# One queue for the first loads, another order of transfers and statistics, and a new order of work on TensorE

## The chip, the cores and the metric

The kernel runs on one core of one Trainium2 chip. Its time is the device time of one execution, in microseconds. The engines are TensorE (PE: matmuls; PEld: its weight loads), VectorE (DVE), ScalarE (ACT), GpSimd (POOL) and SyncE (SP). SP issues DMAs and computes nothing; ACT can issue DMAs too.

## The reference

A layer norm without scale feeds two branches, and both are added to the input. S is 2048, D 448, H 16 heads of 28, F 1792; all inputs are bfloat16.

```python
xn = layernorm(x)                                   # (1, 2048, 448)
# branch A: linear attention with a softmax feature map
q, k, v = split(xn @ wqkv)                          # 16 heads of 28
pq, pk = q @ w_phi, k @ w_phi                       # per head
phi = lambda p: concat(softmax(p), softmax(-p))     # 56 features
kv, z = phi(pk).T @ v, phi(pk).sum(tokens)
A = ((phi(pq) @ kv) / (phi(pq) @ z + 1e-6)) @ wo
# branch B: feed-forward
B = silu(xn @ w1) @ w2
out = x + A + B
```

## The kernel before

**Tiles.** The 2048 tokens are 16 tiles of 128. D is contracted in pieces of 128 rows (the last piece overlaps the third, so that its upper 64 rows are the remainder); matmuls with 64 rows run in pairs on the two halves of PE.

**How the program is ordered.** Nothing is emitted directly. Every instruction is recorded as an operation with its engine, an assumed duration, the tiles it reads and writes, and a name; `schedule` (L218) then orders each engine by a list schedule over these assumptions, and waits are derived from the data dependences. All matmuls are emitted by one helper line (L469), all activations by L489, all plain loads by L503, all DMA transposes by L562. Two things bind the order by hand: `chain` (L883) makes the named operations of one engine follow each other, and the text `PLAN` (L334) lists the blocks of PE after the head; `strict` (L943) makes PE follow it.

**The loads.** x comes as x0, x1, x2 (tiles 2 and 3), x4, x8 and x12 (four tiles each). w1 comes in pieces named by their first column: w1_0 (256 columns, rows 0 to 383) with w1_0r (the remaining 64 rows, inside the last 128), w1_256r (those rows for columns 256 to 767), w1_256, w1_512, w1_768, w1_1280. wv, w2 and wo follow. w1_256 and w1_512 are issued by ACT, together with w_phi; all others by SP.

**The head.** Tiles 0 to 3 are normalised on DVE (`ln_tile`, L600): bnst (statistics), bnag (aggregate), ve on ACT (square root), rstd (reciprocal), xn (subtract and scale). PE transposes them through PSUM (tr0a, tr0, tr1, tr2, tr3), and ACT (tiles 0 to 2: ev0a, ev0, ev1, ev2) or DVE (tile 3: ev3) copies the result to `xnT`. Blocks F0, F1 and F2 of the up-projection are computed tile by tile in between: in the list at L905 the word `12` is block 1, tile 2; `10a` is block 1, tile 0, contraction steps one and two, `10b` the third.

**Tiles 4 to 15** are normalised with POOL in place of ACT and transposed by DMA, two tiles at a time: xnT_dma5 moves tiles 4 and 5, xnT_dma7 tiles 6 and 7, up to xnT_dma15. Eight transposes wT_dma0 to wT_dma7 bring q's and k's weights, which the fold multiplies with w_phi on PE. The chain at L932 fixes the order of x8, x12, wT and xnT on SP; SP issues in order and stops where an operation has to wait.

**Words of PLAN.** `aF12@0` is the first half of up-projection block 12 into banks 0 and 1, `bF12` its second half and eviction; block n holds column pair n mod 7 of token group n div 7 (512 tokens, so blocks 7 to 13 need tiles 4 to 7). v, k and q are projections of two tiles, f the fold, K the sums over tokens (they need POOL's `phik`), M their masking, s the scaling of q's features on POOL with their DMA transposes (`phqT` in the code, phT<-RA in the profile), U the attention product of a tile, after which DVE normalises (den, rden, o) and SP transposes o by DMA (vaug<-vaug in the profile). W is the output projection's three full pieces, R or r the remaining 64 rows, paired over tiles of odd and even slots by `finish_tiles` (L874), followed by the eviction (`out_ev`) and the store. F and Y are parts of the down-projection: `F4@0:2` is two of 14 steps of tile 4 in bank 0. E is the last tile.

Of the kernel before, what the change touches and what calls it, by code (L numbers as in the profile page):

```python
# [8 lines left out]
ACTF = mybir.ActivationFunctionType  # L9
# [131 lines left out]
class _Prog:  # L141
# [76 lines left out]
    def schedule(self):  # L218
# [55 lines left out]
        while done < n:  # L274
# [56 lines left out]
TAIL = {"act": 110.0, "dve": 85.0, "pool": 45.0}  # L331
SIGNAL = {("act", "pe"): 60.0, ("act", "dve"): 40.0, ("dve", "pe"): 100.0, ("dve", "sp"): 30.0, ("dve", "dve"): 34.0,
          ("pool", "pe"): 100.0}
PLAN = """aF3@4 bF3 aF6@0 aF4@2 bF6 av2@4 bF4 av0@6 bv2 bv0 aF12@0 aF8@2 aF9@4 bF8 bF9 aF11@6 bF12 bF11 f2@24 aF13@0 aF10@6 bF13  # L334
bF10 f0@24 aF5@0 aF7@6 bF5 bF7 ak2@4 bk2 av12@6 ak14@2 av10@0 bv12 bk14 bv10 ak4@4 av14@6 bk4 ak0@2 bv14 ak6@0 bk0 av8@4
bk6 ak8@6 bv8 bk8 Y2@3:2 Y2:12 av4@1 av6@6 ak10@4 bv4 bv6 bk10 ak12@2 aq4@0 bk12 K0-4 bq4 aq6@4 aq8@2 bq6 K4-8 aq0@0 bq8
aF17@4 bq0 bF17 s4 aF14@2 K8-10 bF14 aF19@0 K10-12 bF19 aF16@4 K12-16 aF23@2 bF16 bF23 aF27@0 M aF24@5 bF27 bF24 aF20@2
aF25@0 bF20 bF25 s6 aF26@5 aF22@3 bF26 bF22 aF21@0 aF18@5 bF21 aF15@2 bF18 aq12@0 s8 bF15 bq12 aq2@4 s0 U5 U4@6 Y1@3:3
Y1:2 Y1:9 F4@0:2 bq2 aq14@6 aq10@1 bq14 bq10 Y3@3:4 F8@5:9 Y3:10 F8:2 F8:1 F8:2 U8@1 F6@4:12 s2 s10 F4:3 F4:6 U7 F5@3:7
F4:3 U0@2 W4 s12 U6@6 F6:2 U9 U3@1 Y0@2:2 W8 F5:5 F5:2 U13 W5 r4 r5 Y0:8 U11 U12@6 F10@1:2 F10:6 U2@0 Y0:4 F10:1  # L340
F12@6:11 F7@2:3 W6 U10@0 F7:8 F7:3 F11@0:1 F11:4 F12:3 F10:5 W3@3 W0@7 W7 s14 W12 W10 R6,10,8,7 R3,0,12 F11:9 F14@4:7 U1
F13@5:1 F13:4 F13:9 F14:7 U14 W13 F9@2:3 W1@3 F9:4 U15 F9:7 W9 W11 W2@7 W14 R14,1 R9,2 R11,13 F15@61:14 E15"""


def bass_parallel_sum__linear_kernel_hedgehog__dense_activation_silu__prompt_kernel(
# [10 lines left out]
    S, D, H, DH, FF = 2048, 448, 16, 28, 1792  # L356
# [7 lines left out]
    KF = 384  # L364
# [11 lines left out]
    with es:  # L376
# [27 lines left out]
        w1_sb = flat[:, 0:4 * FF].rearrange("p (k f) -> p k f", k=4)  # L404
# [20 lines left out]
        warm_act = sb("warm_act", [128, 4], F32)  # L425
# [30 lines left out]
        def d_act(n):  # L456
            return n / 1.2 + 60.0
# [30 lines left out]
        def act(dst, src, func, n, name, scale=1.0, table=None, **keys):  # L488
            P.op("act", d_act(n), lambda e: e.activation(dst, src, func, scale=scale),  # L489
                 reads=[src], writes=[dst], table=table, name=name, **keys)  # L490
# [8 lines left out]
        def load(dst, src, name, eng="sp", lat=1700.0):  # L499
            n = 2  # L500
            for _, cnt in list(dst.ap):
                n *= cnt
            P.dma(lambda e: e.dma_start(out=dst, in_=src), n / 280.0, writes=[dst], name=name, eng=eng, lat=lat)  # L503
# [40 lines left out]
        load_x(1, 2)  # L544
        load_x(2, 4)
        load_w1(0, 256)
        load(w1_sb[:, 3, 256:768], B_w1[D - 128:D, 256:768], "w1_256r")
        for c in (256, 512):
            load(w1_sb[:, 0:3, c:c + 256], B_w1[0:KF, c:c + 256].rearrange("(k p) f -> p k f", p=128), f"w1_{c}", "act")
        load_x(4, 8)  # L550
        load_w1(768, 1280)
        load_w1(1280, FF)
# [47 lines left out]
        def ln_tile(t):  # L600
            xs = x_sb[:, t, :]
            sl = t % NXN
            P.op("dve", 590, lambda e: e.bn_stats(st6[:, t, :], xs), reads=[xs], writes=[st6[:, t, :]], name=f"bnst{t}", okeys_w=["ln"])  # L603
            P.op("dve", 170, lambda e: e.bn_aggr(mv[:, t, :], st6[:, t, :]), reads=[st6[:, t, :]], writes=[mv[:, t, :]], name=f"bnag{t}",
                 okeys_w=["ln"])
            if t < 4:
                P.op("act", 220, lambda e: e.activation(ve[:, t:t + 1], mv[:, t, 1:2], ACTF.Sqrt, bias=epst[:]),
                     reads=[mv[:, t, 1:2], epst[:]], writes=[ve[:, t:t + 1]], name=f"ve{t}", table="sqrt", okeys_r=["sq"])
                P.op("dve", 120, lambda e: e.reciprocal(rstd[:, t:t + 1], ve[:, t:t + 1]),
                     reads=[ve[:, t:t + 1]], writes=[rstd[:, t:t + 1]], name=f"rstd{t}")  # L610
            else:
                P.op("pool", 200, lambda e: e.tensor_scalar(ve[:, t:t + 1], mv[:, t, 1:2], EPS_LN, None, ALU.add),
                     reads=[mv[:, t, 1:2]], writes=[ve[:, t:t + 1]], name=f"ve{t}")
                P.op("pool", 570, lambda e: e.tensor_tensor(rstd[:, t:t + 1], ve[:, t:t + 1], neghalf[:], ALU.pow),  # L614
                     reads=[ve[:, t:t + 1], neghalf[:]], writes=[rstd[:, t:t + 1]], name=f"rstd{t}")

            def norm(dst, c0, c1, dur, tag=""):
                P.op("dve", dur, lambda e: e.tensor_scalar(dst, x_sb[:, t, c0:c1], mv[:, t, 0:1], rstd[:, t:t + 1], ALU.subtract, ALU.mult),  # L618
                     reads=[xs, mv[:, t, 0:1], rstd[:, t:t + 1]], writes=[dst], name=f"xn{t}{tag}")

            dstx = xnT[:, t, :, :]
            if t >= XN_DMA0:
                norm(xn_sb[:, sl, 0:KF], 0, KF, 370)
                norm(xn_sb[:, sl, KF:512], D - 128, D, 250)
                if t % 2:
                    dma_t(xnT[:, t - 1:t + 1, :, :].rearrange("p i k c -> p (i k) c"),
                          xn_sb[:, sl - 1:sl + 1, :].rearrange("p i c -> p (i c)"), 2200.0 if t < 8 else 1600.0, f"xnT_dma{t}", 1350.0)
                return

            def turn_over(k0, k1, b, tag):  # L630
                tps = bank16[b][:, 128 * k0:128 * k1].rearrange("p (k c) -> p k c", k=k1 - k0)
                transposes([(tps[:, kt - k0, :], xn_sb[:, sl, KS[kt]:KS[kt] + 128]) for kt in range(k0, k1)], f"tr{tag}")
                if t < 3:
                    act(dstx[:, k0:k1, :], tps, ACTF.Identity, 128 * (k1 - k0), f"ev{tag}")
                else:
                    copy(dstx[:, k0:k1, :], tps, 128 * (k1 - k0), f"ev{tag}")

            if t == 0:
                norm(xn_sb[:, sl, 0:256], 0, 256, 290, "a")
                norm(xn_sb[:, sl, 256:D], 256, D, 275)  # L640
                turn_over(0, 2, 4, "0a")
                turn_over(2, 4, 5, "0")
            else:
                norm(xn_sb[:, sl, 0:D], 0, D, 390)
                turn_over(0, 4, (7, 4, 5)[t - 1], str(t))
# [147 lines left out]
        UB = 7  # L793
        yts = {int(w[1:].split(":")[0].split("@")[0]) for w in PLAN.split() if w[0] == "Y"}
        ob_cnt = [0]
# [87 lines left out]
        def chain(names):  # L883
            byname = {o.name: o for o in P.ops}
            for a, b in zip(names, names[1:]):
                byname[b].odeps.add(byname[a].id)
                byname[b].odeps -= byname[b].deps
# [3 lines left out]
            ln_tile(t)  # L891
        fold()
        act(warm_act[:], ones_bf[:, 0:4], ACTF.Silu, 4, "silu_table", table="silu", okeys_w=["sq"])
        chain("bnst0 bnag0 bnst1 bnag1 rstd0 xn0a xn0 rstd1 xn1 bnst2 bnag2 bnst3 bnag3 rstd2 xn2 rstd3 xn3 ev3".split())
        chain("wphi warm_act w1_256 w1_512 ve0 ve1 ev0a ev0 ev1 ve2 ve3 ev2 silu_table".split())
        fold_loads()

        chunk = [(fp, c) for c in range(NCH) for fp in range(FP)]
# [3 lines left out]

        head = [F(0, 0), F(1, 2), F(2, AUX)]
        seq = []
        for word in "tr0a tr0 tr1 00a 00b 10a 01 10b 11 tr2 20 tr3 21 02 12 22 03 13 23".split():  # L905
            if word[0] == "t":
                seq.append(word)
                continue
            f, t = int(word[0]), int(word[1])
            n0 = len(P.ops)  # L910
            head[f][0](t * 128, t * 128 + 128, {"": (0, 1, 2), "a": (0, 1), "b": (2,)}[word[2:]])
            for n, o in enumerate(P.ops[n0:]):
                o.name = f"F{word}_{n}"
                seq.append(o.name)
# [3 lines left out]
            f[3]()  # L918
        for t in range(4, 8):
            ln_tile(t)  # L920
        chain("ev3 bnst4".split())
        block_mask(mask2[:], 2 * DH, 2)
        memset(vaug[:, :, :, DH], 1.0, 2150, "vaug1")
        def k_block(t, b0):
# [4 lines left out]

        for t in range(8, NT):  # L930
            ln_tile(t)
        chain("x8 wT_dma0 wT_dma1 wT_dma2 xnT_dma5 x12 xnT_dma7 wT_dma3 wT_dma4 wT_dma5 wT_dma6 wT_dma7 xnT_dma9 xnT_dma11 xnT_dma13 xnT_dma15 w2 "  # L932
              "wo0 wor0 wo1 wor1".split())
        memset(phq[:, :, :, KP:128], 0.0, 400, "phq0")
        late = max(o.id for o in P.ops if o.name == "xn15")
# [15 lines left out]
        open_kind = {"F": F, "v": v_block, "k": k_block, "q": q_block}  # L951
        for word in PLAN.split():
            n0 = len(P.ops)
            kind, arg = word[0], word[1:]
            if kind == "a":
                t, b = map(int, arg[1:].split("@"))
                blocks[arg[0], t] = open_kind[arg[0]](t, b)
                blocks[arg[0], t][2](0)
            elif kind == "b":
                f = blocks[arg[0], int(arg[1:])]  # L960
# [147 lines left out]
```

## Time and profile before

| | us |
|---|---|
| median of 8 runs | 150.23 (149.49 to 151.22) |
| the profiled execution's own time | 150.5 |
| its span in the trace | 149.2 |
| PE busy | 143.9 (96%) |
| DVE, ACT, POOL busy | 90.8, 71.2, 71.4 |

The granted clock of PE is full speed in every slice of the page. The span is from the first to the last recorded instruction. Times in the text are microseconds from its start. A matmul's recorded duration overlaps with the next one's, so the durations of PE rows are not added; starts are compared instead. A DMA row has the time from its issue to its landing. For the text, a hole is a stretch in which PE has nothing to do because it waits.

### The profile page before, as it was taken

What the parts mean: (1) busy time and instruction counts of PE and PEld (TensorE: products, weight loads), DVE (VectorE), ACT (ScalarE), POOL (GpSimd) and SP (SyncE); (2) the same over time, 40 slices, a digit from 0 to 9 for tenths busy, and PEclk for the clock granted to TensorE, in tenths of its full rate; (3) what the DMA queues carried; (4) which work ended last, traced back from release to release, by engine and by line L of the source; (5) the groups of instructions that cost most, each with busy time, mean ns of one, the idle gap of its engine ahead of it and who ended that gap; (6) DMA issues with size and microseconds to landing.
All of it is one profiled execution on the core that took longest, in us unless ns stands there. A gap on an engine that the chain in (4) does not pass through costs nothing.

```text
span 149.2 us, 3651 instructions
## 1 busy us (share of the span) xinstructions
PE 143.9 (96%) x1540; PEld 80.5 (54%) x1540; DVE 90.8 (61%) x189; ACT 71.2 (48%) x88; POOL 71.4 (48%) x82
## 2 busy tenths in 40 slices
PE   7799969999999999999999999999999999999994
PEld 7594435554554456656444454455565555455563
DVE  1968897343399966604995018998388620482255
ACT  3567755557999659899656685930000000000000
POOL 7107566510069999998899800896910000000000
PEclk9999999999999999999999999999999999999999
DMA  5999994989600000000089673068786984051135
GB/s 121 318 362 227 205 204 74 195 184 354 196 2 4 0 2 4 4 0 4 3 161 143 119 141 67 7 116 163 77 189 143 184 78 70 25 190 35 40 80 173
DMA packets 45297, 17.42 MB, mean 117 GB/s; under 512 B 36960, under 2 KB 44896, under 8 KB 45280
## 3 DMA queue, kind: packets, MB, share of 16 engines
q1 hardware_dynamic: 41712, 14.99, 49.3%
q10 hardware_dynamic: 3568, 2.20, 4.7%
q8 instruction: 12, 0.20, 0.6%
q14 instruction: 5, 0.04, 0.1%
HBM read 6.56 MB, written 1.84 MB: 56 GB/s over the span
## 4 chain that ended last, share of the span: by engine, by line
PE 93%; DMA 3%; issue 1%; SPq 1%; DVE 1%
PE psum L469 92%; DMA phT<-in_B_w_dram 3%; SPq L503 1%; DVE x_sb L856 1%; PE psum L484 0%
## 5 line engine op out<-in xcount | busy, mean ns | idle before, releaser
L469 PE MATMUL psum<-xnT,phT 64*128 64x512 bf16 (+1 forms) x428 | 44.9, 350 | 2.0 <-issue 1.2
L469 PE MATMUL psum<-w_sb,hT 128*128 128x448 bf16 (+1 forms) x238 | 45.4, 341 | 0.0
L489 ACT ACTIVATE hT<-psum 128x1024 bf16<-128x1024 f32 x28 | 27.2, 1023 | 15.6 <-PE psum L469 15.6
L469 PEld LDWEIGHTS psum<-xnT,phT 64*128 64x128 bf16 (+1 forms) x428 | 21.3, 95 | 21.9 <-issue 1.6
L774 POOL TENSOR_TENSOR RA<-Ek_sb,Rec 128x896 bf16<-128x896 bf16 x16 | 27.1, 1723 | 11.5 <-DVE Rec L739 11.5
L469 PEld LDWEIGHTS psum<-w_sb,hT 128*128 128x128 bf16 x238 | 22.2, 98 | 18.3 <-issue 1.5
L738 DVE TENSOR_REDUCE Rec<-Ek_sb 128x32 f32<-128x896 bf16 (+1 forms) x20 | 24.2, 1250 | 12.8 <-POOL Ek_sb L496 7.1
L469 PE MATMUL psum<-Wqk,xnT 64*128 64x432 bf16 x224 | 23.2, 343 | 0.1
L489 ACT ACTIVATE Ek_sb<-psum 128x864 bf16<-128x864 f32 x24 | 20.1, 910 | 2.6 <-PE psum L469 2.2
L748 POOL TENSOR_TENSOR Ek_sb<-Ek_sb,Rec 128x896 bf16<-128x896 bf16 x8 | 13.3, 1696 | 9.3 <-ACT phT L489 9.3
L469 PEld LDWEIGHTS psum<-Wqk,xnT 64*128 64x128 bf16 x224 | 10.7, 94 | 10.1 <-PE psum L469 0.9
L834 DVE TENSOR_SCALAR den<-psum 128x16 f32<-128x16 f32 x16 | 2.6, 162 | 19.7 <-PE psum L469 19.6
L748 POOL TENSOR_TENSOR phT<-phT,Rec 128x896 bf16<-128x896 bf16 x8 | 13.3, 1697 | 0.0
L856 DVE TENSOR_TENSOR x_sb<-psum,x_sb 128x448 bf16<-128x448 f32 (+1 forms) x13 | 7.1, 583 | 9.6 <-PE psum L469 9.6
L469 PE MATMUL psum<-wv,xnT 64*128 64x448 bf16 x112 | 12.4, 349 | 0.0
L603 DVE BATCH_NORM_STATS2 st<-x_sb 128x6 f32<-128x448 bf16 x16 | 9.7, 604 | 3.5 <-DMA x_sb<-in_A_x_dram 3.4
L469 PE MATMUL psum<-wo_sb,vaug 128*128 128x448 bf16 (+1 forms) x51 | 10.7, 341 | 0.0
L841 DVE TENSOR_TENSOR vaug<-psum,rden 128x448 bf16<-128x448 f32 x16 | 10.0, 625 | 0.7 <-DVE rden L836 0.2
L618 DVE TENSOR_SCALAR RA<-x_sb,mv,rstd 128x384 bf16<-128x384 bf16 (+4 forms) x29 | 8.9, 347 | 1.3 <-POOL rstd L614 1.2
L738 DVE TENSOR_REDUCE Rec<-phT 128x64 f32<-128x1792 bf16 x4 | 7.9, 1988 | 2.6 <-ACT phT L489 2.6
L489 ACT ACTIVATE vaug<-psum 128x896 bf16<-128x896 f32 x8 | 7.2, 927 | 3.3 <-PE psum L469 2.9
L739 DVE RECIPROCAL Rec<-Rec 128x32 f32<-128x32 f32 (+1 forms) x24 | 8.6, 392 | 0.1
(51 smaller groups left out, 105.0 us busy)
## 6 DMA issues: line engine op xcount, KB each, us to landing
out_dram<-x_sb ACTq DMA_DIRECT2D x15, 112.0 KB, 1.7
w_sb<-in_B_w_dram SPq DMA_DIRECT2D x1, 1568.0 KB, 7.7
x_sb<-in_A_x_dram SPq DMA_DIRECT2D x3, 448.0 KB, 5.1
phT<-in_B_w_dram SPq DMA_DIRECT2D x2, 384.0 KB, 6.0
wo_sb<-in_A_wo_dram SPq DMA_DIRECT2D x2, 336.0 KB, 8.5
phT<-in_B_w_dram ACTq DMA_DIRECT2D x2, 192.0 KB, 4.2
phT<-in_B_w_dram SPq DMA_DIRECT2D x3, 128.0 KB, 5.7
wv<-in_A_wqkv_dram SPq DMA_DIRECT2D x1, 336.0 KB, 6.6
```

The costliest lines, as they stand in the source:

```text
L469: r = e.matmul(dst, lhsT, rhs, start=st, stop=sp, skip_group_check=True)
L489: P.op("act", d_act(n), lambda e: e.activation(dst, src, func, scale=scale), reads=[src], writes=[dst], table=table, name=name, **keys)
L503: P.dma(lambda e: e.dma_start(out=dst, in_=src), n / 280.0, writes=[dst], name=name, eng=eng, lat=lat)
L603: P.op("dve", 590, lambda e: e.bn_stats(st6[:, t, :], xs), reads=[xs], writes=[st6[:, t, :]], name=f"bnst{t}", okeys_w=["ln"])
L618: P.op("dve", dur, lambda e: e.tensor_scalar(dst, x_sb[:, t, c0:c1], mv[:, t, 0:1], rstd[:, t:t + 1], ALU.subtract, ALU.mult), reads=[xs, ...
L738: P.op("dve", 50 + 967 * n, lambda e: e.tensor_reduce(R2, E4, AXL.X, ALU.add), reads=[E4], writes=[R2], name="Ssum")
L739: P.op("dve", 135 + 210 * n, lambda e: e.reciprocal(R2, R2), reads=[R2], writes=[R2], name="Rrec")
L748: P.op("pool", 1700, lambda e: e.tensor_tensor(E3, E3, Rk[:, :, None].broadcast_to([128, 32, DH]), ALU.mult), reads=[E3, Rk], writes=[E3], ...
L774: P.op("pool", 1700, lambda e: e.tensor_tensor(dst, Eq, Rq.rearrange("p (c j) -> p c j", c=CC)[:, :, :, None].broadcast_to([128, CC, 4, DH ...
L834: P.op("dve", 190, lambda e: e.tensor_scalar(den[:, uq, :], U3[:, :, DH], EPS_DEN, None, ALU.add), reads=[U3[:, :, DH]], writes=[den[:, uq ...
L841: P.op("dve", 620, lambda e: e.tensor_tensor(o3, U3[:, :, 0:DH], rden[:, uq, :, None].broadcast_to([128, H, DH]), ALU.mult), reads=[U3[:, ...
L856: P.op("dve", d_dve(cs.stop - cs.start), lambda e: e.tensor_tensor(res[:, cs], ob, addend[:, cs], ALU.add), reads=[ob, addend[:, cs]], wri ...
```

## The change

Six edits go together.

1. w1_256 and w1_512 are issued by SP, and w1_256r stands between them. SP's order is now x0, x1, x2, w1_0, w1_0r, w1_256, w1_256r, w1_512, x4, and so on.
2. The eviction of tile 2 (ev2) is two activations of 256 columns, ev2a and ev2.
3. In the head's list, block column 0 of F1 is no longer split, and tile 2's three blocks are split by contraction steps (`02a 12a 22a 02b 12b 22b`).
4. The chain on DVE is tied together: bnst4 stands before ev3, and bnag4 after it.
5. On SP, x12 is issued after wT_dma2 and before xnT_dma5; before, it stood between xnT_dma5 and xnT_dma7.
6. PLAN is replaced. Up to the fold it holds as many blocks as before, with F9, F8, F10 and F13 as the first of token group 1. Later, the order of Y, F, U and W words differs, and the remainders R run as one single tile and seven pairs, where before there were two singles and groups of 4, 3, 2, 2 and 2.

```diff
-PLAN = """aF3@4 bF3 aF6@0 aF4@2 bF6 av2@4 bF4 av0@6 bv2 bv0 aF12@0 aF8@2 aF9@4 bF8 bF9 aF11@6 bF12 bF11 f2@24 aF13@0 aF10@6 bF13
-bF10 f0@24 aF5@0 aF7@6 bF5 bF7 ak2@4 bk2 av12@6 ak14@2 av10@0 bv12 bk14 bv10 ak4@4 av14@6 bk4 ak0@2 bv14 ak6@0 bk0 av8@4
...
-F4:3 U0@2 W4 s12 U6@6 F6:2 U9 U3@1 Y0@2:2 W8 F5:5 F5:2 U13 W5 r4 r5 Y0:8 U11 U12@6 F10@1:2 F10:6 U2@0 Y0:4 F10:1
-F12@6:11 F7@2:3 W6 U10@0 F7:8 F7:3 F11@0:1 F11:4 F12:3 F10:5 W3@3 W0@7 W7 s14 W12 W10 R6,10,8,7 R3,0,12 F11:9 F14@4:7 U1
-F13@5:1 F13:4 F13:9 F14:7 U14 W13 F9@2:3 W1@3 F9:4 U15 F9:7 W9 W11 W2@7 W14 R14,1 R9,2 R11,13 F15@61:14 E15"""
+PLAN = """aF3@4 bF3 aF4@2 bF4 aF6@6 av2@0 av0@4 bF6 bv0 bv2 aF9@2 aF8@4 aF10@6 bF9 aF13@0 bF8 bF13 bF10 f2@24 aF5@0 aF7@6 bF5 bF7
+f0@24 aF12@0 aF11@6 bF12 bF11 ak2@4 bk2 av12@6 av10@0 ak14@2 bv12 bk14 bv10 ak4@4 av14@6 bk4 ak0@2 bv14 bk0 ak8@0 ak6@4
...
+F4:6 U8 F7@3:10 F7:3 U9@4 F7:1 F4:2 Y0:4 W5 W4 U3 W7 F9@6:1 aq14@4 R4 R5,7 bq14 F9:2 U1 F8@2:2 F8:12 U2 F9:11 s12 U12@4
+F6@5:5 W9 W3@1 U10@3 W1@0 F10@7:5 F6:9 W8 F14@3:3 F10:9 W6 W10 s14 R6,10 R3,9 R1,8 U13@4 F14:11 U14 F12@1:2 F11@2:8 U0@5
+W2@4 U11 F12:12 U15@0 F11:6 F13@6:5 W12 W14 W11 F13:9 W0@5 W13 R12,11 R14,0 R2,13 F15@70:14 E15"""
...
         load_w1(0, 256)
-        load(w1_sb[:, 3, 256:768], B_w1[D - 128:D, 256:768], "w1_256r")
         for c in (256, 512):
-            load(w1_sb[:, 0:3, c:c + 256], B_w1[0:KF, c:c + 256].rearrange("(k p) f -> p k f", p=128), f"w1_{c}", "act")
+            load(w1_sb[:, 0:3, c:c + 256], B_w1[0:KF, c:c + 256].rearrange("(k p) f -> p k f", p=128), f"w1_{c}")
+            if c == 256:
+                load(w1_sb[:, 3, 256:768], B_w1[D - 128:D, 256:768], "w1_256r")
         load_x(4, 8)
...
-                if t < 3:
+                if t == 2:
+                    act(dstx[:, 0:2, :], tps[:, 0:2, :], ACTF.Identity, 256, "ev2a")
+                    act(dstx[:, 2:4, :], tps[:, 2:4, :], ACTF.Identity, 256, "ev2")
+                elif t < 3:
...
-        chain("bnst0 bnag0 bnst1 bnag1 rstd0 xn0a xn0 rstd1 xn1 bnst2 bnag2 bnst3 bnag3 rstd2 xn2 rstd3 xn3 ev3".split())
-        chain("wphi warm_act w1_256 w1_512 ve0 ve1 ev0a ev0 ev1 ve2 ve3 ev2 silu_table".split())
+        chain("wphi warm_act ve0 ve1 ev0a ev0 ev1 ve2 ve3 ev2a ev2 silu_table".split())
...
-        for word in "tr0a tr0 tr1 00a 00b 10a 01 10b 11 tr2 20 tr3 21 02 12 22 03 13 23".split():
+        for word in "tr0a tr0 tr1 00a 00b 10 01 11 tr2 20 tr3 21 02a 12a 22a 02b 12b 22b 03 13 23".split():
...
-        chain("ev3 bnst4".split())
+        chain("bnst0 bnag0 bnst1 bnag1 rstd0 xn0a xn0 rstd1 xn1 bnst2 bnag2 bnst3 bnag3 rstd2 xn2 rstd3 xn3 bnst4 ev3 bnag4".split())
...
-        chain("x8 wT_dma0 wT_dma1 wT_dma2 xnT_dma5 x12 xnT_dma7 wT_dma3 wT_dma4 wT_dma5 wT_dma6 wT_dma7 xnT_dma9 xnT_dma11 xnT_dma13 xnT_dma15 w2 "
+        chain("x8 wT_dma0 wT_dma1 wT_dma2 x12 xnT_dma5 xnT_dma7 wT_dma3 wT_dma4 wT_dma5 wT_dma6 wT_dma7 xnT_dma9 xnT_dma11 xnT_dma13 xnT_dma15 w2 "
               "wo0 wor0 wo1 wor1".split())
```

More of the change, by code (lines that the diff above doesn't have):

```diff
@@ L333 @@
           ("pool", "pe"): 100.0}
-PLAN = """aF3@4 bF3 aF6@0 aF4@2 bF6 av2@4 bF4 av0@6 bv2 bv0 aF12@0 aF8@2 aF9@4 bF8 bF9 aF11@6 bF12 bF11 f2@24 aF13@0 aF10@6 bF13
-bF10 f0@24 aF5@0 aF7@6 bF5 bF7 ak2@4 bk2 av12@6 ak14@2 av10@0 bv12 bk14 bv10 ak4@4 av14@6 bk4 ak0@2 bv14 ak6@0 bk0 av8@4
[L336 to L339, printed above, removed]
-F4:3 U0@2 W4 s12 U6@6 F6:2 U9 U3@1 Y0@2:2 W8 F5:5 F5:2 U13 W5 r4 r5 Y0:8 U11 U12@6 F10@1:2 F10:6 U2@0 Y0:4 F10:1
-F12@6:11 F7@2:3 W6 U10@0 F7:8 F7:3 F11@0:1 F11:4 F12:3 F10:5 W3@3 W0@7 W7 s14 W12 W10 R6,10,8,7 R3,0,12 F11:9 F14@4:7 U1
-F13@5:1 F13:4 F13:9 F14:7 U14 W13 F9@2:3 W1@3 F9:4 U15 F9:7 W9 W11 W2@7 W14 R14,1 R9,2 R11,13 F15@61:14 E15"""
+PLAN = """aF3@4 bF3 aF4@2 bF4 aF6@6 av2@0 av0@4 bF6 bv0 bv2 aF9@2 aF8@4 aF10@6 bF9 aF13@0 bF8 bF13 bF10 f2@24 aF5@0 aF7@6 bF5 bF7
+f0@24 aF12@0 aF11@6 bF12 bF11 ak2@4 bk2 av12@6 av10@0 ak14@2 bv12 bk14 bv10 ak4@4 av14@6 bk4 ak0@2 bv14 bk0 ak8@0 ak6@4
+av6@6 bk6 bv6 bk8 Y2@2:1 Y2:9 Y2:1 Y2:3 av4@6 av8@0 ak10@4 bv8 bv4 bk10 ak12@2 aq4@0 bk12 K0-2 K2-4 bq4 aq6@4 aq8@2 bq6
+K4-8 aq0@0 bq8 s4 bq0 aF17@4 K8-10 bF17 aF14@2 K10-12 aF19@0 bF14 bF19 aF16@4 K12-16 aF23@2 aF27@0 bF23 bF27 bF16 M
+aF20@2 aF25@0 bF20 aF24@4 bF25 bF24 aF26@2 aF21@0 s6 aF18@6 aF22@4 bF21 s8 bF18 bF22 bF26 aF15@0 aq2@6 bF15 aq10@4 bq2
+aq12@2 bq10 bq12 Y1@0:14 s0 F5@1:4 Y3@6:11 F5:4 s2 F4@2:6 U4 Y3:3 s10 F5:1 F5:5 U5@3 U7@5 U6@4 Y0@6:1 Y0:3 Y0:2 Y0:4
+F4:6 U8 F7@3:10 F7:3 U9@4 F7:1 F4:2 Y0:4 W5 W4 U3 W7 F9@6:1 aq14@4 R4 R5,7 bq14 F9:2 U1 F8@2:2 F8:12 U2 F9:11 s12 U12@4
+F6@5:5 W9 W3@1 U10@3 W1@0 F10@7:5 F6:9 W8 F14@3:3 F10:9 W6 W10 s14 R6,10 R3,9 R1,8 U13@4 F14:11 U14 F12@1:2 F11@2:8 U0@5
+W2@4 U11 F12:12 U15@0 F11:6 F13@6:5 W12 W14 W11 F13:9 W0@5 W13 R12,11 R14,0 R2,13 F15@70:14 E15"""
 def bass_parallel_sum__linear_kernel_hedgehog__dense_activation_silu__prompt_kernel(
```

## The prediction

> **What bounds the kernel now.** I read the chain of work that ended last first, in order of time, because it says where TensorE (PE) stood still.
>
> ```profile
> 2.19 4.90 DMA phT<-in_B_w_dram
> ...
> 7.14 1.51 PE psum L469 x24
> ...
> 9.44 3.77 PE psum L469 x53
> ...
> 13.26 6.71 PE psum L469 x64
> 19.96 1.17 issue
> 21.14 14.83 PE psum L469 x150
> ...
> 36.01 110.84 PE psum L469 x1184
> 146.87 0.77 DVE x_sb L856 x2
> ```
>
> PE carries 92.5% of it. It waits in two places only: until 7.14 for the first piece of w1 (issued at 2.19, landed 4.90 later), and from 19.96 to 21.14. From 21.14 to the last eviction at 146.87 there is no hole. So time can be won only at those two places, or by taking work off PE; it is lost where a new hole opens.
>
> The second hole says only "issue". At 21.14 begins block F12, the first that reads token tiles 4 to 7 transposed. The SyncE (SP) queue in order of time shows how they come:
>
> ```profile
> 7.90 4.09 SPq L562 DMA_TRANSPOSE Y_sb<-in_A_wqkv_dram  x3
> 13.54 2.12 SPq L562 DMA_TRANSPOSE xnT<-RA  x1
> 15.70 0.58 SPq L503 DMA_DIRECT2D x_sb<-in_A_x_dram  x1
> 16.32 1.24 SPq L562 DMA_TRANSPOSE xnT<-RA  x1
> ```
>
> The second xnT transpose (tiles 6 and 7) is issued at 16.32 and, in the DMA view of that moment, lands 4.7 later: 21.04, and PE starts 0.1 after. I take this to be the wait; the page does not name it. The busy table (columns: stretch, PE, PEld, DVE, ACT and POOL, clock, DMA share, GB/s) shows what the queue did meanwhile:
>
> ```profile
> 14.00:15.00 1.00, 1.00 (x14) 0.41 (x12) 0.40 (x3) 1.00 (x3) 0.56 (x1) 1.00 0.41 20
> ...
> 16.50:17.00 0.50, 0.50 (x8) 0.27 (x6) 0.49 (x1) 0.50 (x1) 0.35 (x2) 1.00 1.27 259
> ...
> 17.25:18.00 0.75, 0.75 (x10) 0.38 (x8) 0.75 (x3) 0.34 (x2) 0.67 (x3) 1.00 0.35 43
> 18.00:19.00 1.00, 1.00 (x14) 0.49 (x12) 1.00 (x5) 0.95 (x1) 0.92 (x3) 1.00 0.91 354
> ```
>
> Almost nothing moves at 14 to 15 (the load x8 is finishing, transposes stand behind it), and again at 17.25 to 18, where the load x12 follows a transpose. In between the rate is 250 to 370.
>
> **The change, part by part.**
>
> **1. w1_256 and w1_512 go from ACT's queue to SP's, behind w1_0.** On ACT they are issued at 1.32 and 1.79 and land 3.7 and 4.8 later (5.0 and 6.6); w1_0, issued at 2.19, lands at 7.1. Loads land in order of issue across both queues, so 384 KB stand ahead of w1_0. At the 348 to 365 GB/s of 5 to 8 us that is 1.1 us: w1_0 lands near 6.0. PE cannot use all of it: tile 0's last eviction ends at 6.22 and tile 1's transposes at 6.34, so the first 24 matmuls start near 6.25, 0.9 earlier. Next come tiles 2 and 3, whose normalisation on VectorE (DVE) ends at 7.96 and 8.46 and hardly moves: their statistics start at 5.91, just after the tile-1 work ends at 5.82. Tile 2's transposes can start at 8.0 instead of 8.50; its eviction (0.60 before, now two halves of 0.38 that PE may follow one by one) lets block column 2 begin near 9.0 instead of 9.6. The head is 0.55 us shorter. That w1_512 now lands later (near 7.6, all bytes being the same) costs nothing: its first reader follows tile 2's transposes, after 8.0.
>
> SP issues two loads more, 0.47 each (1.35 for three), so whatever stands behind w1_256 on SP issues 0.95 later: x4, the other w1 pieces, wv, x8 and the first three wT transposes. Here a rule can be weighed. By the row, x4 lands 5.1 after issue and x8 8.2 after, against 2.2 for the first load: they wait in the line of bytes, not for SP. The Trainium skill (DMA: Bandwidth & Descriptors, Issuing engines are not separate DMA queues) says that issuing from several engines saves only the sequencer's time to issue. By that rule alone dropping ACT would cost 0.95 on every later load; by the row nothing, since the line is full. I take nothing.
>
> **2. x12 goes ahead of xnT_dma5.** The three wT transposes end on SP near 12.95 (11.99 plus 0.95), x12 takes 0.58, and xnT_dma5 issues near 13.55, as before (13.54): its producer, tile 5, is ready by then. xnT_dma7 follows at about 15.7, 0.6 earlier than 16.32. What counts is the line of transfers. Landings before: third wT 16.9 (10.73 plus 6.2), xnT_dma5 17.7 (13.54 plus 4.2), x12 19.9 (15.70 plus 4.2), xnT_dma7 21.0. The steps are 0.8, 2.2 and 1.1, together 4.1. In the new order the same three pieces stand between the third wT and the same end: 21.0 again. It gets better only if x12 is cheaper when issued early. Its bytes alone, 448 KB at 354 GB/s, take 1.3 instead of 2.2, which gives 20.1; but the stretch at 17.25 to 18.00 looks like the price of a copy behind a transpose, and it will now stand behind the third wT. Bounds 20.1 and 21.4 (a second such stop before xnT_dma5); I take 20.9, near the row.
>
> A second rule speaks for much more. The Trainium skill (DMA: Bandwidth & Descriptors, Anatomy of one DMA) gives a fixed 2.0 us plus bytes at 436 GB/s for a DMA, measured there on another issue path. For xnT_dma7's 256 KB that is an estimate of 2.6: issued at 15.7 it would land at 18.3, before PE arrives. Then the hole would vanish and the gain would be the head's 0.55 plus 1.17. The row says 4.7 from issue to landing, because the line ahead is not empty. The row decides.
>
> PE, 0.55 early, reaches the block (now F9, after the same amount of work as F12 before: three F blocks and two v blocks) near 19.4 and waits until 21.0. **The head's gain is swallowed**; the end moves by what xnT_dma7 moves, 0.15.
>
> **3. bnst4 ahead of ev3 on DVE.** bnst4 waits for x4 (3.67 plus 5.1: 8.8) with ev3 behind it, then takes 0.62; ev3 (0.42) ends near 9.8, as before (9.90). Tile 3's first reader on PE comes 18 short matmuls (57 ns each) after 9.0, at 10.0. Hidden; if x4 came 0.5 late, PE would lose 0.3 here and get it back in the hole of part 2. The tile-4 to 7 work that follows runs 0.6 earlier, but its transposes wait in the line anyway.
>
> **4. The new PLAN.** Matmul counts are unchanged but for the paired rests of the output projection: before, tiles 5 and 4 go singly, then groups of four, three and three times two: 2+2+2+3 = 9 slots. Now tile 4 alone and seven pairs: 8. A 448-wide matmul takes 0.19 (21 in 4.14 at 132.33): minus 0.19.
>
> Then the new waits. I laid the rows' durations along each queue in the new order. Early: PE can move up by at most 0.95 before K12-16 meets POOL, whose last phik ends at 68.84 against 69.79 on PE; and fold f2 (27.29) must not pass wT_dma7 (22.82 plus 3.8: 26.6). Neither binds a move of 0.15. Late: seven o transposes (1.31 apart on SP) stand ahead of the phq transpose of tiles 12 and 13, which is issued near 112.2, while PE reaches U12 near 117.4. How long do they take?
>
> ```profile
> phT<-RA SPq DMA_TRANSPOSE x11, 4.2
> ...
> vaug<-vaug SPq DMA_TRANSPOSE x16, 2.5
> ```
>
> With 4.2 it lands at 116.4; three output stores run at the same time, and the o transpose beside two stores at 113.00 took 3.5 instead of 2.5, so 116.9 to 117.6. W5 and W7 (PE near 107.9 and 109.3) have landings at 106.5 and 107.8, W10 0.8 of slack, W11 0.5. Bounds 0 and 1.2 of stall; I take 0.15.
>
> **Sum.** Head 0 (covered by the hole), xnT_dma7 -0.15, one slot -0.19, new waits +0.15: -0.2. On the profiled execution that is 150.5 to 150.3 (its span 149.2, 1.3 around it); its 150.5 lies 0.3 above the median of 150.23, so the same step on the median gives **150.0**.
>
> **The rivals.**
>
> *The line gets shorter (faster).* x12's early issue takes out the stop at 17.25, xnT_dma7 lands at 20.1 to 20.3 and PE is 0.75 to 0.95 earlier there. For it: the first slow packets follow x12's late issue. Against: the stop comes where the kind of transfer changes. With the slot: -0.95 to -1.1, 149.1 to 149.3.
>
> *A late transpose (slower).* The place is the phq pair of tiles 12 and 13. The row that speaks for it, of the pair issued at 115.71 before:
>
> ```profile
> phT<-RA SPq DMA_TRANSPOSE x1, 6.2
> ```
>
> It cost nothing there, with some 14 us of slack; now there is one. At 6.2 from 112.2 it lands at 118.4, PE stands 1.0 and the sum is +0.65; with the o transposes before it late as well (3.5 to 4.9 in several rows) +1.2 or more: 150.9 to 151.6. It decides from a landing 1.4 us over the quiet 4.2 plus the stores. Against: nine of the eleven take 4.4 or less.
>
> *x12 in front hurts (slower).* It holds up xnT_dma5 and xnT_dma7 and a second stop opens between: 21.6 to 22.2, +0.6 to +1.1: 150.8 to 151.3.
>
> **How the numbers follow.** A measurement of this kernel can tell about 0.5% from no change, 149.5 to 151.0. My forecast 0.44, the shorter line 0.28, the late transpose 0.20, x12 in front 0.08. So faster 0.28, same 0.44, slower 0.28. My own case spans 149.6 to 150.6; with the ends of both sides, 149.1 to 151.3.
>
> **What would show it.** Right: first head matmuls near 6.25; a hole of about 1.5 us near 19.4, ended by xnT_dma7 near 20.9; PE dense from there, no hole over 0.3 from 107 to 118. Wrong: the hole is gone or under 0.8 (the line), or a hole over 0.7 opens at U12 or a W word (late transposes), or at K12-16 before POOL.

## The result and the profile after

The changed kernel takes 151.96 us, median of 11 runs (151.18 to 152.78). Beside 32 runs of the kernel before on the same chip (149.98; 149.47 to 153.06) the ratio is 1.0108, with a 95% interval of 1.0078 to 1.0138: it is slower by 1.1%, some 1.6 us (the medians lie 2.0 apart), where 150.0 was forecast with a range to 151.3. A second measurement (after_again) gave 151.49 and 1.0107 [1.0064, 1.0150]. The profiled execution took 151.32 (span 150.0), 0.8 more than the one of before and 0.6 under its own median. Some executions take 1 to 2% longer, most of them at a lower granted clock, so a ratio can differ from the quotient of two medians, and the profiled executions of loads_on_sp, two_queues and act_late are such longer ones.

The chain of work that ended last, of the changed kernel:

```profile
3.21 4.16 DMA phT<-in_B_w_dram
...
7.42 1.31 PE psum L469 x18
...
15.10 5.20 PE psum L469 x50
20.29 0.69 issue
20.98 6.22 PE psum L469 x56
...
35.94 75.11 PE psum L469 x912
...
111.07 1.69 DVE x_sb L860 x3
112.75 0.13 DVE den L838
...
113.49 4.99 DMA phT<-RA
...
118.53 29.14 PE psum L469 x220
...
147.69 0.78 DVE x_sb L860 x2
```

There were two waits; now there are three. The first ends at 7.42 instead of 7.14, and by another piece: six matmuls of block 0 did start at 6.31, but w1_256 lands only at 7.37. The second still ends where it did (20.98 against 21.14). The third is new: PE stands idle for 0.90 before U12, until the phq transpose of tiles 12 and 13 has landed. Counted from start to start it loses 1.07 there: from the first of the 11 matmuls of F9:11 to U12 are 3.15 (115.38 to 118.53), and 2.08 where nothing waits (pair_first, below). At 36 PE is still 0.07 ahead of before (35.94 against 36.01); the last eviction is 0.82 late (147.69 against 146.87). That is the 1.07, less the 0.07 and the 0.19 of the saved slot. So this pair of traces shows the whole of U12's loss, but little of what the late loads cost: that stands in the times below, and in the second trace (after_again), where PE is at 36.46 instead of 35.94.

The SP queue of the changed kernel at the second wait:

```profile
9.24 5.18 SPq L563 DMA_TRANSPOSE Y_sb<-in_A_wqkv_dram  x3
14.47 0.58 SPq L503 DMA_DIRECT2D x_sb<-in_A_x_dram  x1
15.09 3.26 SPq L563 DMA_TRANSPOSE xnT<-RA  x2
```

Its busy table at that place, with the columns of the prediction's:

```profile
15.00:16.00 1.00, 0.94 (x12) 0.43 (x12) 0.29 (x2) 0.99 (x2) 0.00 (x0) 1.00 0.54 86
...
17.25:18.00 0.75, 0.75 (x12) 0.36 (x10) 0.72 (x3) 0.00 (x0) 0.74 (x2) 1.00 0.91 339
```

The stop at 17.25 (43 GB/s before) is gone. The 86 GB/s at 15 to 16 is not that stop in a new place: before has such a low stretch too, while x8 finishes and the wT transposes stand behind it (20 GB/s at 14 to 15); with later loads it comes later. The pair of xnT transposes is issued at 15.09 and 16.40, and the second lands at 20.89.

### The profile page after: what moved, and what is told of

Its sections match the earlier page's. It is cut to its first block, busy times and chain, and to the rows that moved or that the text cites. A ratio compares the mean times of both kernels' runs of the same rounds, so it can differ in the third digit from the quotient of the medians.

```text
span 150.0 us, 3659 instructions
## 1 busy us (share of the span) xinstructions
PE 144.6 (96%) x1540; PEld 80.4 (54%) x1540; DVE 90.4 (60%) x189; ACT 70.9 (47%) x89; POOL 71.4 (48%) x82
## 4 chain that ended last, share of the span: by engine, by line
PE 88%; DMA 6%; DVE 2%; SPq 2%; issue 1%
PE psum L469 88%; DMA phT<-RA 3%; DMA phT<-in_B_w_dram 3%; DVE x_sb L860 2%; SPq L503 1%; PE psum L484 0%; DVE rden L840 0%; SPq L563 0%; DVE den L838 0%; SPq L1069 0%
## 5 line engine op out<-in xcount | busy, mean ns | idle before, releaser
L489 ACT ACTIVATE Ek_sb<-psum 128x864 bf16<-128x864 f32 x24 | 20.3, 915 | 18.7 <-DVE x_sb L860 17.3
L469 PEld LDWEIGHTS psum<-wv,xnT 64*128 64x128 bf16 x112 | 5.4, 94 | 5.3 <-ACT phT L489 0.4
```

What stands on the lines that cost most here:

```text
L469: r = e.matmul(dst, lhsT, rhs, start=st, stop=sp, skip_group_check=True)
```

## The experiments

Ratios are to the kernel before, run on the same chip beside it, with 95% intervals.

### Which part costs: one part undone, one part alone

`old_plan` is the changed kernel with the old text of PLAN; `new_plan` the kernel before with the new one (the whole text is exchanged, so it isn't shown). `loads_on_sp` is the kernel before with edit 1 alone, `x12_first` with edit 5 alone, `all_but_loads` the changed kernel without edit 1 (`...` stands for lines left out, here and in the other code cuts):

```diff
+        load(w1_sb[:, 3, 256:768], B_w1[D - 128:D, 256:768], "w1_256r")
         for c in (256, 512):
-            load(w1_sb[:, 0:3, c:c + 256], B_w1[0:KF, c:c + 256].rearrange("(k p) f -> p k f", p=128), f"w1_{c}")
-            if c == 256:
-                load(w1_sb[:, 3, 256:768], B_w1[D - 128:D, 256:768], "w1_256r")
+            load(w1_sb[:, 0:3, c:c + 256], B_w1[0:KF, c:c + 256].rearrange("(k p) f -> p k f", p=128), f"w1_{c}", "act")
...
-        chain("wphi warm_act ve0 ve1 ev0a ev0 ev1 ve2 ve3 ev2a ev2 silu_table".split())
+        chain("wphi warm_act w1_256 w1_512 ve0 ve1 ev0a ev0 ev1 ve2 ve3 ev2a ev2 silu_table".split())
```

> The changed kernel with the PLAN of before: loads, chains, head list and the place of x12 stay as changed. Theory A (the loss is in the new PLAN, at U12, where PE waits for the transpose of tiles 12 and 13): the loss is gone, the time is that of the kernel before, 149.6 to 150.3, and the trace has no hole after 22 us. Theory B (the loss comes from the loads in one queue, which land 0.4 to 0.8 us later in the trace of the changed kernel): the loss stays, 151.3 to 152.0.

> The kernel before with the new PLAN alone. Theory A: as slow as the changed kernel, 151.3 to 152.2, with a hole of 0.7 to 1.5 us at U12 near 118. Theory B: the time of the kernel before, less the 0.2 of the saved slot, 149.6 to 150.1.

> The kernel before with only w1_256 and w1_512 on SP (and w1_256r between them); head list, chains on DVE, x12 and PLAN as before. Theory C (one queue moves less than two: the line has gaps that ACT's loads had filled): x4 lands at 9.6 to 10.6 instead of 8.8, x8 at 16.0 or later instead of 15.6, xnT_dma7 at 21.4 to 22.0 instead of 21.0, and the time grows by 0.4 to 0.9 us, to 150.3 to 150.8. The prediction's step (the line is full, the move costs nothing): xnT_dma7 at 21.0 and 149.7 to 150.1.

> The kernel before with only x12 ahead of xnT_dma5. Theory D (issued early, x12 costs its bytes and no more): third wT 16.9, x12 18.3, xnT_dma5 19.4, xnT_dma7 20.6; the hole at F12 shrinks from 1.2 to 0.7, the time falls by 0.4, to 149.5. The prediction's step (the same three pieces, the same end): xnT_dma7 at 20.9 to 21.0, time 149.8 to 150.0.

> The changed kernel with w1_256 and w1_512 back on ACT, in the order of before; all other parts as changed. Theory C: x4 lands near 9.0 again, the wait of PE for ev3 behind bnst4 (0.7 to 1.1 us in three traces with the loads on SP) falls under 0.2, xnT_dma7 lands near 20.6, and the hole at U12 is what is left: 150.4 to 151.0. If the reordered statistics (bnst4 ahead of ev3) are at fault by themselves, that wait stays and the time is 151.2 or more.

> The changed kernel once more, for a second trace of it: its profiled run was at the low end of its times (151.32 against a median of 151.96). Theory A: the hole at U12 is there again, and where the run is slower it is longer: 0.9 to 1.8 us. Theory B: the difference to the first trace lies before 22 us.

> loads_on_sp once more, beside late_issue and act_late on one chip, because its first profile was of a disturbed execution. If the single queue costs what the first times said: 0.4 to 0.8% slower than before, x4 landing 0.8 or more later than before's 8.8, the hole before F12 at 21.1 or later by 0.5 to 1.0. If the first times were chance: within 0.3% of before.

| kernel | median us | ratio |
|---|---|---|
| old_plan | 150.91 | 1.0054 [1.0030, 1.0078] |
| new_plan | 151.06 | 1.0051 [1.0027, 1.0076] |
| loads_on_sp | 151.22 | 1.0063 [1.0033, 1.0093] |
| loads_on_sp_again | 151.20 | 1.0054 [1.0026, 1.0082] |
| x12_first | 149.92 | 0.9988 [0.9951, 1.0026] |
| all_but_loads | 150.39 | 1.0010 [0.9980, 1.0040] |
| after_again | 151.49 | 1.0107 [1.0064, 1.0150] |

So there are two causes of about half a per cent each: the single queue, and the new PLAN. x12 in front neither helps nor hurts by an amount that can be measured. In x12_first xnT_dma7 lands at 19.94, 1.1 earlier than before, and the hole at 21 nearly closes (0.3); but PE then reaches the fold before wT_dma7 is there. The end of that stretch in its chain:

```profile
24.11 2.56 DMA Y_sb<-in_A_wqkv_dram
...
26.80 8.66 PE psum L469 x94
```

Before, the fold began at 27.29, so 0.5 of the 1.1 is left in this trace (its end is at 146.37 instead of 146.87), and the times do not resolve it.

The single queue alone costs what the second wait grows by, in its second trace (loads_on_sp_again) beside that of before. Its chain there:

```profile
13.07 6.71 PE psum L469 x64
19.77 2.25 issue
22.02 14.83 PE psum L469 x150
```

PE reaches the block 0.2 earlier than before (19.77 against 19.96), as it should with a quicker head, and gets on 0.88 later (22.02 against 21.14): xnT_dma7 lands at 21.93 instead of 21.05. The last eviction moves by the same 0.88 (147.75). By the medians it is 1.05 (151.20 against 150.15). In the changed kernel x12 in front gives part of this back: xnT_dma7 lands at 20.89 in the first trace and at 21.12 in after_again, against 19.82 in all_but_loads.

### Why the single queue costs: SP's time, or late bytes

`late_issue` leaves w1_256 and w1_512 on ACT and gives SP two tiny loads, so that all that follows is issued 0.95 later. `act_late` leaves SP alone and makes ACT's two loads wait for x0. `two_queues` and `u12_later_two` are the changed kernel with U12 moved (below) and two queues again, the first in the new order of use, the second in the old one.

```diff
 late_issue, against the kernel before
+        spare = sb("spare", [128, 2, 32], BF16)
...
+        for n in range(2):
+            load(spare[:, n, :], B_w1[0:128, 32 * n:32 * n + 32], f"spare{n}")
         load_x(4, 8)
...
 act_late, against the kernel before
+        P.ops[[o.name for o in P.ops].index("w1_256")].deps.add(next(o.id for o in P.ops if o.name == "x0"))
 two_queues, against the changed kernel
-        load_w1(0, 256)
+        load_w1(0, 256, "act")
-        for c in (256, 512):
...
+        load(w1_sb[:, 0:3, 256:512], B_w1[0:KF, 256:512].rearrange("(k p) f -> p k f", p=128), "w1_256", "act")
+        load(w1_sb[:, 3, 256:768], B_w1[D - 128:D, 256:768], "w1_256r")
+        load(w1_sb[:, 0:3, 512:768], B_w1[0:KF, 512:768].rearrange("(k p) f -> p k f", p=128), "w1_512")
...
```

> The kernel before with two tiny loads (128 rows of 64 B each, read by nobody) on SP ahead of x4; w1_256 and w1_512 stay on ACT. It takes from the single queue only this: everything behind on SP is issued 0.95 later. If SP's time to issue is the loss of the single queue: x4 lands 0.6 to 1.0 later than the 8.8 of before, x8 and xnT_dma7 0.5 to 0.9 later, and the time is 0.4 to 0.7% up, like loads_on_sp. If the line of bytes hides it, as my prediction had it: x4 at 8.8 to 9.1, time within 0.2% of before, and the loss lies in the bytes that are not asked for early or in the queue itself.

> The kernel before with ACT's w1_256 and w1_512 waiting for x0 (landed 3.07), so that they are issued near 3.1 and 3.6, as late as SP issues them in the changed kernel, but from ACT: SP's own issues keep their times. If the loss of the single queue is that the bytes of these two pieces are asked for 1.8 later while the transfers run dry near 3.0: fewer bytes by 8 us, x4 near 9.4 or later, time 0.3 to 0.7% up. If it is SP's time to issue: x4 at 8.8 to 9.1 and no change in time, or a gain of up to 0.3%, since w1_0 comes earlier.

> As u12_later_two, but the order of use over two queues: ACT issues w1_0 and w1_256, SP w1_0r, w1_256r and w1_512. If the loss of the single queue is the loss of the second queue: x4 lands at 8.8 to 9.3 as before (9.6 to 10.7 with one queue), PE's head starts near 6.3, and the time is that of u12_later_two or up to 0.3 less. If it is the order itself (w1_512 behind w1_0) that makes x4 and x8 late: x4 at 9.6 or later, and the time is 0.4 to 0.9 over u12_later_two.

> The changed kernel with w1_256 and w1_512 back on ACT and U12 moved behind F6@5:5 and W9. My theory of two causes (later loads, and U12's late pair of tiles 12 and 13): both are gone, what is left is one slot less, x12 ahead and the new head: no hole over 0.3 from 107 to 120, 0.6 to 1.0 us faster than before, 149.2 to 149.6. Rival, that the new PLAN costs something beyond U12 (other words that wait, or the rests in pairs): 149.9 to 150.4, as with the U12 hole.

| kernel | median us | ratio |
|---|---|---|
| late_issue | 150.08 | 0.9989 [0.9960, 1.0018] |
| act_late | 154.23 (6 runs, from 151.63) | 1.0175 [1.0102, 1.0249] |
| two_queues | 149.52 | 0.9942 [0.9918, 0.9966] |
| u12_later_two | 149.58 | 0.9973 [0.9942, 1.0004] |

SP's time to issue costs nothing that the times show: the median of late_issue is that of before. Its x4, issued at 4.63 instead of 3.67, lands at 9.28, within what kernels with the old loads show (8.69 to 9.52). One sign that was named for the other answer is there all the same: xnT_dma7 lands at 21.67, 0.6 later than before. It does not come from SP's queue. This profiled execution (151.19) is longer than its median, and its head is slow:

```profile
7.51 2.74 PE psum L470 x24
```

Before, these 24 took 1.51. They start 0.107 apart instead of 0.056, as in the first 5 us of before; the trace records full clock from 10.41 only (from 4.0 to 7.0 in the ten other traces that record it). So tile 5 was normalised late, at 15.23, and SP, done with the wT transposes at 12.89, waited for it until 15.26.

Two queues don't save a kernel whose second queue starts late either: act_late loses at least as much as the single queue. How much more is not shown. Its ratio rests on three runs, from 151.63 to 153.87, and in its trace w1_512 landed 8.30 after its issue, PE waited until 11.82 for it, and meanwhile the granted clock fell (40 slices of 3.84 us, in tenths of full speed):

```profile
PEclk9985799999999999999999999999999999999999
```

It is 0.50 from 10.25 to 17.08. The 63 matmuls from 11.82 on take 7.04 there and 4.38 before (8.88 to 13.26), so 2.7 of the 4.25 us by which this trace ends later are clock and not loads.

What the losing kernels have in common is in the busy table. Its last column is GB/s. Two rows of the kernel before:

```profile
3.00:3.50 0.50, 0.50 (x8) 0.50 (x7) 0.43 (x1) 0.00 (x0) 0.43 (x3) 1.00 1.02 307
...
5.00:6.00 1.00, 0.89 (x9) 0.41 (x8) 0.88 (x5) 0.44 (x2) 0.00 (x0) 1.00 1.14 348
```

The first of them, of late_issue:

```profile
3.00:3.50 0.50, 0.50 (x8) 0.50 (x6) 0.46 (x1) 0.00 (x0) 0.43 (x3) 1.00 1.15 316
```

Of the changed kernel:

```profile
3.00:3.50 0.50, 0.50 (x8) 0.50 (x6) 0.40 (x1) 0.00 (x0) 0.43 (x3) 1.00 0.94 86
...
5.00:6.00 1.00, 0.89 (x9) 0.38 (x8) 0.96 (x5) 0.41 (x3) 0.00 (x0) 1.00 0.71 203
```

And the first of act_late:

```profile
3.00:3.50 0.50, 0.50 (x8) 0.50 (x6) 0.49 (x1) 0.00 (x0) 0.43 (x3) 1.00 1.07 113
```

With two loads asked for at 1.32 and 1.79 by ACT the transfers run at over 300 GB/s by 3.0. Where ACT had asked for nothing but w_phi before 3.0, they fall to 86 to 113 for half a microsecond (83 in loads_on_sp_again), although SP has asked for 640 KB by then (x0, x1, x2 and w1_0) and no more than half of that has moved. Summed over the half microseconds up to 8.0, 1840 KB moved before and 1780 in late_issue, against 1540 in the changed kernel and 1580 in loads_on_sp_again: 260 to 300 KB, 0.7 to 0.8 us at 360 GB/s, of the size of the 0.88 above. The 18 traces of this case divide the same way: the seven with one queue have 1520 to 1590 KB by 8.0, act_late 1450, the ten with two queues from the start 1780 to 1900. Two queues in the new order of use win it back: two_queues against u12_later (one queue, otherwise the same kernel) is 149.52 against 150.97, and u12_later_two (the old order) has 149.58.

What is shown, then, is that the loss goes with these two pieces being asked for late; SP's time to issue alone does not bring it, and neither does the new order of use. That the missing bytes are the way by which it reaches xnT_dma7 is read from the tables and fits in size; no run tests it apart. Why SP's queue alone, with loads still under way, leaves the transfers short at 3.0, and why the rate of the changed kernel falls again at 5 to 6 while that of act_late does not (308 GB/s), stays open.

### Why U12 waits: evictions, the transpose, or SP's queue

`u12_later` is the changed kernel with U12 two words later. `r57_later` takes the paired rests R5,7, and with them two of the three evictions and stores, out of the way. `pair_first` is new_plan with the pair of tiles 12 and 13 ahead of the o transposes of U9 and U3 on SP.

```diff
 u12_later
-U2 F9:11 s12 U12@4 F6@5:5 W9 W3@1
+U2 F9:11 s12 F6@5:5 W9 U12@4 W3@1
 r57_later
-R4 R5,7 bq14 F9:2 U1 F8@2:2 F8:12 U2 F9:11 s12 U12@4
+R4 bq14 F9:2 U1 F8@2:2 F8:12 U2 F9:11 s12 U12@4 R5,7
 pair_first, against new_plan
                 scale_rows(int(arg), False)
+                if arg == "12":
+                    for o in [o for o in P.ops if o.name == "oT_dma"][-4:]:
+                        o.odeps.add(P.ops[-1].id)
```

> The changed kernel with one word of PLAN moved: U12@4 comes after F6@5:5 and W9, 8 matmuls or 1.5 us later. Theory A: the transpose has landed by then, the hole of 0.9 is gone or under 0.3, and the time falls by 0.7 to 1.5 us against the changed kernel, to 150.5 to 151.2. Theory B: no change, 151.6 to 152.2. If the hole only moves to W9 or a later word, a whole group of transposes is late and not this one alone.

> The changed kernel with the word R5,7 moved from ahead of bq14 to behind U12. If the pair of tiles 12 and 13 is late because its issue on SP stands behind an o transpose whose den, rden and o wait on DVE behind the three output evictions of R4 and R5,7: the pair is issued near 112.4, over 0.8 earlier than in the changed kernel, lands 4.2 to 4.6 later, the hole at U12 is under 0.3, and the time is 0.5 to 1.0 under the changed kernel's, 151.0 to 151.5. If the transpose itself is slow whatever DVE does (over 5 from issue to landing): the hole stays near 0.9 and the time near 152.

> The kernel before with the new PLAN (as new_plan, which was 0.5% slower than before), and on SP the phq transpose of tiles 12 and 13 ahead of the o transposes of U9 and U3. In new_plan its two POOL products were long done, but it stood behind seven o transposes that SP issued without a pause. If SP's queue is the cause of U12's hole: the pair is issued near 109.5 to 110.2 (112.77 in new_plan), lands before 115.5, the hole of 1.32 at U12 is gone, no W word waits more than 0.3, and the time is 0.5 to 1.0 under new_plan's: 149.6 to 150.3. If the new PLAN costs elsewhere too: the hole goes and the time stays at 150.7 or more.

| kernel | median us | ratio | the pair issued, landed | PE idle before U12 |
|---|---|---|---|---|
| changed kernel | 151.96 | 1.0108 [1.0078, 1.0138] | 113.49, 118.48 | 0.90 |
| u12_later | 150.97 | 1.0068 [1.0044, 1.0092] | 114.68, 119.49 | none |
| r57_later | 152.51 | 1.0137 [1.0094, 1.0180] | 114.39, 118.81 | 0.80 |
| new_plan | 151.06 | 1.0051 [1.0027, 1.0076] | 112.77, 118.22 | 1.16 |
| pair_first | 149.93 | 0.9989 [0.9961, 1.0016] | 110.10, 115.68 | none |

My theory for r57_later fell. The chain of the changed kernel leads from the pair back through den to three evictions on DVE (1.69 together), and I read it as written. But with two of them moved away the pair came no earlier, and the hole stayed. The SP queue says what really stands before it. In the changed kernel:

```profile
102.85 10.52 SPq L563 DMA_TRANSPOSE vaug<-vaug  x7
113.49 3.14 SPq L563 DMA_TRANSPOSE phT<-RA  x1
```

And in pair_first:

```profile
101.48 8.51 SPq L562 DMA_TRANSPOSE vaug<-vaug  x5
110.10 1.84 SPq L562 DMA_TRANSPOSE phT<-RA  x1
```

In the changed kernel the pair's two products on POOL were done at 104.18. From then to 113.38 SP does nothing but issue o transposes, end to end, and the pair is the eighth in line. Put ahead of the last two it is issued 2.7 earlier than in new_plan, the hole is gone (from start to start it cost 1.33 in new_plan), and with it the whole cost of the new PLAN (1.0051 to 0.9989). It still took 5.58 to land, beside three stores; in r57_later, with one store, it took 4.41, much like the two pairs before it in the changed kernel (4.24 and 4.41).

### A version that is faster than both

The hole at 21 can be filled with work that needs no late tile: block 5 of token group 0, which the kernel before runs at the end of that stretch, comes ahead of block 12. `hole_filled` does it with the halves of blocks side by side, `filled_apart` without.

```diff
 hole_filled, against the kernel before (words of PLAN)
-bv2 bv0 aF12@0 aF8@2 aF9@4 bF8 bF9 aF11@6 bF12 bF11 f2@24 aF13@0 aF10@6 bF13 bF10 f0@24 aF5@0 aF7@6 bF5 bF7
+bv2 bv0 aF5@0 bF5 aF12@2 bF12 aF8@4 bF8 aF9@6 bF9 aF13@0 f2@24 bF13 aF10@6 bF10 f0@24 aF11@0 aF7@6 bF11 bF7
 filled_apart, against the kernel before
+bv2 aF5@0 bv0 bF5 aF12@2 aF8@4 bF12 aF9@6 bF8 aF13@0 bF9 f2@24 aF10@6 bF13 bF10 f0@24 aF11@0 aF7@6 bF11 bF7
 both
-aF16@4 K12-16 aF23@2 bF16 bF23
+aF16@4 aF23@2 bF16 K12-16 bF23
```

> The kernel before with PLAN changed in two places: block F5, which needs only tiles 0 to 3, goes into the hole ahead of F12 (F11 goes to F5's old place, and f2 behind half of F13), and K12-16 comes behind F23's first half and F16's second. If the hole at 20 to 21 us is what swallows the head and if PE's work sets the end (all theories), it is gone and the time falls by 0.8 to 1.1 us, to 148.8 to 149.2. If POOL or the fold's weights set the end, the hole comes up again at the fold near 26 or at K12-16 near 69, and the time stays within 0.3 of before.

> The kernel before with two changes in PLAN: block 5 of token group 0 comes ahead of block 12, so that the first block that reads tiles 4 to 7 starts 1.7 us later, and the halves of two blocks never follow each other directly; K12-16 stands three words later. If the hole before the first block of token group 1 is worth its length and the 0.22 gaps of the run before came from halves standing side by side: no hole near 21, no 0.22 gaps from 21 to 31, 0.6 to 0.9 us faster than before (149.2 to 149.4). If moving blocks only moves the wait to the fold or to K12-16: a new hole there of 0.5 or more, and no change.

hole_filled took 150.54, 1.0033 [1.0005, 1.0062]; filled_apart 149.40, 0.9946 [0.9922, 0.9970]. The chain of hole_filled:

```profile
13.64 7.37 PE psum L469 x70
...
21.06 1.70 PE psum L469 x14
...
22.81 1.70 PE psum L469 x14
```

And of filled_apart:

```profile
13.12 13.42 PE psum L469 x126
```

In the first the long wait is gone, but where the second half of a block (8 matmuls) comes directly behind its first (6) the chain breaks, every 14 matmuls, at 21.06, 22.81, 24.56, 26.31 and 30.57. From 21.06 to 22.81 it takes 1.75 for 14, where the 56 from 20.98 to 27.23 of the changed kernel take 6.25, 1.56 for 14: some 0.2 lost at each. (The 13.26 of the kernel before is such a turn too, of F3; the new PLAN has a second one, of F4, at 15.10 in the changed kernel, which its second wait covers.) It also had its head 0.5 later than filled_apart. In the second PE runs from 13.12 to the fold without a stop. It and two_queues are faster than the kernel before, by 0.8 to 0.9 us by their ratios and by 0.4 to 0.6 by the medians (149.40 and 149.52 against 149.95). The two were not tried together.

## Why the prediction was wrong, point by point

**1. The loads.** The head was right in its first half: w1_0 landed at 5.88 (forecast 6.0), and the first matmuls began at 6.31 (6.25). It failed on the piece that it never costed. I followed w1_0, which gained, and w1_512, which had time to spare, but not w1_256, which block column 1 needs after six matmuls of column 0: it went from 5.04 to 7.37. The run at the head's end starts at 13.32 against 13.26: the 0.55 is not there.

The sentence that failed is "by the row nothing, since the line is full". The row (x4 5.1 after issue) shows that the line was full with ACT's two loads in it. It does not show that it would stay full when they come later, and the changed kernel's 86 GB/s at 3.0 says that it did not. The rule weighed there (the Trainium skill, DMA: Bandwidth & Descriptors, Issuing engines are not separate DMA queues) gave 0.95 for each later load. x4 indeed came 0.8 later in the profile (9.58), and 1.8 later in after_again (10.60). But the rule gets near the number for another reason: it says that issuing from several engines saves only the sequencer's time, and late_issue, which takes that time and nothing else, is not slower. The measurement decides against both readings. By the ratios the changed kernel against all_but_loads is 1.0108 over 1.0010, about 1% or 1.5 us; alone the single queue is 0.5 to 0.6%. The difference of the two is within the intervals.

**2. x12 ahead of xnT_dma5.** xnT_dma7 was forecast at 20.9 and landed at 20.89, but not for the reason given. The stop was to move behind the third wT. It went away: x12 alone brings xnT_dma7 to 19.94, below my lower bound of 20.1 and near the 20.1 to 20.3 of the rival that the line gets shorter, and the late loads take 0.9 back. That the two errors meet at 20.9 is luck. PE arrived at 20.29 and not at 19.4, so the hole was 0.69 instead of 1.5, with the same end.

**3. bnst4 ahead of ev3.** Hidden, if x4 comes at 8.8: that condition is what failed. In the profiled run x4 at 9.58 cost nothing, but that is the exception: in the six other traces with one queue x4 lands at 10.46 to 10.71. In after_again the chain of work goes through it:

```profile
10.63 0.63 DVE st L604
11.26 0.33 DVE xnT L493
...
11.63 2.60 PE psum L469 x29
```

PE waits 1.0 for ev3, which stands behind bnst4, which waits for x4; in three other traces with this chain and one queue (old_plan, u12_later and r57_later) it waits 0.6 to 1.1. The forecast gave 0.3 for 0.5 of delay and said that the hole before F9 gives it back; in after_again it does (that hole is 0.1 there), but behind it the fold waits 0.3 for an eviction on ACT, with its last weights landed only at 27.61, and its start is at 27.75 instead of 27.23. This may be why the late loads cost more in the changed kernel than alone; no run takes this edit alone away.

**4. The new PLAN.** The +0.15 of new waits is the second term of the sum that was mis-sized; it measured 0.90 of idle time, 1.07 from start to start, within the bounds of 0 to 1.2. The cause was named: seven o transposes stand ahead of the pair. I counted them at 1.31 apart; they took 10.52 together, 1.50 apart, so the pair was issued at 113.49 instead of 112.2. Then it took 4.99, within the 4.7 to 5.4 that I had with the stores. The landing of 118.48 and the wait of 0.9 are those of the rival that I called a late transpose (118.4 and 1.0), to which I gave 0.20, though most of the delay is a later issue and not the 6.2 to landing that it rested on.

**The sum.** Forecast -0.2; measured +1.6. By the ratios: late loads in this kernel +1.0%, U12 +0.4% (the changed kernel over u12_later, or all_but_loads over u12_later_two), the rest -0.3% (u12_later_two). The rival gave 151.6 at most, because it left the loads at nothing; each of the two errors alone, as new_plan and loads_on_sp measured them (151.06 and 151.22), would have stayed inside the range to 151.3.

## What to carry to other kernels

A queue that is full in the profile tells what it costs to issue later *into it*, not what happens when you take away what fills it: before moving loads, ask which bytes are asked for in the first two microseconds. For each piece that lands later, find its first reader, not only for the pieces that the change is about. And before trusting a chain that runs through an engine, look at the queue that issues: one that issues end to end for 10 us is itself the resource, and a transfer that was ready 9 us earlier only needs a better place in it.

## What the runs showed of the hardware that was not expected

- Two loads on a second queue within the first 2 us go with 260 to 300 KB more in the first 8 us; 0.95 of later issue on SP's queue does not show in the time.
- SP's issue of a transpose is not a fixed 1.31: of seven in a row five took 1.26 to 1.28, one 1.70 and one 2.22, and the pair behind them held SP for 3.14.
- The phq transpose of tiles 12 and 13 takes 4.8 to 5.6 to land beside three output stores (eight of the nine traces with the new PLAN) and 4.4 beside one. That the stores are the cause is not shown: the last pair took 5.70 in the changed kernel with no store beside it.
- Two halves of one up-projection block directly behind each other cost PE some 0.2 at the turn (0.44 between two starts instead of 0.21): five times in hole_filled from 21 on, and not in filled_apart at these places, where halves of other blocks stand between.
- A wait of PE can be followed by half the clock. In act_late a wait of 2.29 ended at 11.82, and the granted clock was 0.50 from 10.25 to 17.08; in loads_on_sp one of 2.58 ended at 22.49, and it was 0.50 from 23.78 to 27.19. It does not always: after 2.25 in loads_on_sp_again the clock stayed full.
